# Attention with both batches' first blocks at the head of the order, feeding two feed-forward layers on one core

## The chip, the cores and the metric

The kernel runs on one core of a Trainium2 chip. The metric is the device time of one execution in microseconds; lower is better. All times below are of the kernel before, from its timed runs and from one profiled execution.

## The reference, cut to what matters

Attention over two batches of 768 tokens with 8 heads of 64; a query sees the 96 keys up to its own place and the first 8 keys of its batch, with a slope per head as bias. Its output goes through two feed-forward layers of width 512 to 2048 to 512, the first with a softplus, the second with `h * clip(h + 3, 0, 6) / 6`.

```python
def _attn_ref(q, k, v, n_global, n_local):
    scores = scale * np.matmul(q, k.transpose(0, 1, 3, 2))
    is_global = pos[None, :] < int(n_global)
    is_local = (rel >= 0) & (rel < int(n_local))
    keep = is_global | is_local
    dist = np.where(is_global & ~is_local, float(n_local), np.abs(rel))
    scores = np.where(keep, scores - slopes * dist, -1000000000.0)
    a = np.exp(scores - np.max(scores, axis=-1, keepdims=True))
    return np.matmul(a / (np.sum(a, axis=-1, keepdims=True) + 1e-09), v)

def _moe_ref(x, w_in, w_out):
    h = x @ w_in
    return (np.maximum(h, 0.0) + np.log1p(np.exp(-np.abs(h)))) @ w_out

def _moe2_ref(x, w_in, w_out):
    h = x @ w_in
    return (h * np.clip(h + 3.0, 0.0, 6.0) / 6.0) @ w_out
```

## The kernel before, in words

The weights come as 64-bit words and are turned on the chip into a high and a low part, so that three matmuls (low by high, high by low, high by high) give one product. The tokens are cut into 12 blocks of 128, 6 of each batch (`NB`).

*Attention* goes block by block, and a block in two quads of four heads each, so there are 24 quads (k = 0 to 23). A quad has three steps. `att_s` (L494) makes the scores on PE (L519), adds the bias and takes the row minimum of the negated scores on DVE (L525), takes the exponentials with their sums on ACT (L530), and normalises on POOL (L415). `att_t` (L539), twice in a quad, transposes two heads on PE (L553) and copies the result out of its PSUM bank on ACT (L555); from the sixth quad on there is one such bank. `att_v` (L558) multiplies with the values on PE (L571); after a block's second quad it splits the result into `xsh` and `xsl` (ACT L578, DVE L579), the input of the first layer.

The first block of a batch (i = 0) needs only its own keys, so its scores are 128 wide. Every other block needs its own and the previous block's, 256 wide. The keys of three blocks are kept in `kT`, slot n % 3. The first 32 keys of a batch are global: `att_s` copies them at the first block into `gk` (DVE, L503), and copies them from there over the first 32 columns of a block's slot when that block is done (L536), so that the next block finds them in its "previous" slot. The values do the same by a transfer (L584). At a block's first quad, `load_block` (L442) issues the transfers of the next block's queries and keys, and `load_values` (L448) those of its own values, all on SP's queue.

*The lead* (L657) does the first steps with LEAD = 5: the scores of quads 0 to 6, the transposes of 0 to 4, the values of 0 to 3. It also issues matmuls that compute nothing (`warm_up`) and converts six units of weights (`weight_step`, L155; `unit_convert`, L124). A unit's conversion starts with an absolute value on ACT (L140), goes over POOL and DVE, and ends with a subtraction on DVE (L153). Its work buffer `a` is one of the four quarters of the third partial-sum tile `part[2]`, or one of two buffers `wa` (L134 to L138); in the order of the units they go round in sixes.

*The halves* follow in `Layers.run` (L350). An item of the first layer (256 tokens, two chunks of weights) has two halves of 24 matmuls: `first_h` makes `hf`, `first_g` the softplus, `first_o` the product into `accf`. Between the matmuls of a half the steps of attention quads are issued, those of two quads in the first half, of one in each later half: scores and values ahead of the half's first matmul, transposes ahead of the 6th and of the 18th. The order of the items is fixed; the first ones are the first 256 tokens (two blocks), then the next 256. When the attention is done, its pools are closed and the rest of the two layers runs in items of 512 tokens (`item`, `last_items`), which write the output rows (L306, L329).

PE's instructions are in the order in which the program issues them. Those of ACT, DVE and POOL, with a few exceptions, are put in order by a planner at build time, from its own estimates.

## Time and profile before

| | us |
|---|---|
| median of 3 runs | 647.71 (647.69 to 648.22) |
| profiled execution | 649.05 |
| its span on the core | 647.1 |

The page gives for the whole span the busy time of each engine:

| engine | busy us | share |
|---|---|---|
| PE | 624.8 | 97% |
| PEld (weight loads, beside PE) | 513.8 | 79% |
| DVE | 428.9 | 66% |
| ACT | 375.1 | 58% |
| POOL | 151.0 | 23% |

A busy share is a mean over stages that are limited by different things. The views to read are therefore those by stretch of time, and the waits inside a stretch. A row of the timeline says when an instruction started, how long it took, and in brackets how long its engine was idle before it and what ended that.

### The profile page before, as it was taken

To read this page: it belongs to the slowest core of one execution; us is meant where nothing else is said; L and a number is where in the kernel's file an instruction comes from. 1 tells how busy PE (TensorE), PEld (TensorE's weight loads), DVE (VectorE), ACT (ScalarE), POOL (GpSimd) and SP (SyncE) were. 2 spreads that over 40 slices of the span, in tenths; PEclk is the share of its full clock that TensorE was granted. 3 is DMA by queue.
4 is the path that set the end of the run, shared out by engine and by line. 5 is a ranking of instruction groups with operands and counts; after the bars stand their busy time and mean duration, and the time that the engine had idled before them with its cause. 6 is when DMAs were issued, how large, how long until landed. Compare 5 with 4: busy or idle time off the path is not lost.

```text
span 647.1 us, 9643 instructions
## 1 busy us (share of the span) xinstructions
PE 624.8 (97%) x3495; PEld 513.8 (79%) x3496; DVE 428.9 (66%) x903; ACT 375.1 (58%) x786; POOL 151.0 (23%) x192
## 2 busy tenths in 40 slices
PE   7779998999999999999999999999999999999996
PEld 4567887889999888877788888888888888888885
DVE  7988587645799999999989995225833432424251
ACT  6866878674778887686787752326685222222230
POOL 4786364521133234443200400001100000000000
PEclk9989999999999999999999999999999999999999
DMA  8754222011134234433302032000462000001011
GB/s 285 238 158 147 70 75 62 23 25 66 66 116 146 98 130 131 130 99 129 122 10 66 32 131 98 0 1 32 134 208 82 0 1 0 2 1 65 1 66 69
DMA packets 25082, 53.67 MB, mean 83 GB/s; under 512 B 2497, under 2 KB 9153, under 8 KB 25025
## 3 DMA queue, kind: packets, MB, share of 16 engines
q1 hardware_dynamic: 25024, 52.96, 25.3%
q8 instruction: 29, 0.48, 0.3%
q14 instruction: 29, 0.23, 0.1%
HBM read 49.81 MB, written 3.15 MB: 82 GB/s over the span
## 4 chain that ended last, share of the span: by engine, by line
PE 68%; DVE 16%; ACT 7%; POOL 3%; DMA 3%; issue 2%; SPq 0%; ACTq 0%; DVEq 0%
PE acc L200 25%; PE h L200 24%; PE accf L200 6%; PE hf L200 5%; ACT pm L530 3%; PE accz L200 2%; PE hz L200 2%; DVE wa L147 2%; DVE wa L148 2%; PE ptp L553 2%; DVE w L153 2%; POOL wa L143 1%; POOL pm L415 1%; DVE pm L525 1%; DVE part L296 1%
## 5 line engine op out<-in xcount | busy, mean ns | idle before, releaser
L200 PE MATMUL h<-xsh,w 128*128 128x512 f32 x584 | 159.3, 396 | 0.4 <-DVE t L186 0.4
L200 PEld LDWEIGHTS h<-xsh,w 128*128 128x128 f32 x584 | 109.2, 188 | 27.6 <-DVE t L186 1.6
L143 POOL TENSOR_SCALAR wa<-wa 128x512 f32<-128x512 f32 x56 | 74.2, 1329 | 242.4 <-ACT wa L140 242.1
L200 PE MATMUL acc<-w,gh 128*128 128x512 f32 x344 | 108.0, 395 | 0.0
L190 DVE SCALAR_TENSOR_TENSOR t<-t,h 128x512 f32<-128x512 f32 x43 | 29.5, 686 | 81.7 <-ACT t L189 81.7
L200 PE MATMUL h<-xsl,w 128*128 128x512 f32 x292 | 82.4, 395 | 0.0
L192 DVE TENSOR_TENSOR gl<-t,gh 128x512 fp32r<-128x512 f32 x73 | 51.8, 709 | 43.1 <-ACT gh L191 42.8
L189 ACT ACTIVATE t<-h,three 128x512 f32<-128x512 f32 x43 | 29.5, 686 | 87.6 <-PE h L200 87.4
L200 PE MATMUL acc<-gh,w 128*128 128x512 f32 x240 | 78.9, 396 | 0.3 <-DVE part L296 0.2
L200 PEld LDWEIGHTS acc<-w,gh 128*128 128x128 f32 x344 | 64.5, 188 | 15.7
L191 ACT CAST gh<-t 128x512 fp32r<-128x512 f32 x73 | 45.2, 619 | 46.0 <-PE acc L200 22.0
L200 PE MATMUL acc<-w,gl 128*128 128x512 f32 x172 | 68.0, 396 | 0.0
L200 PEld LDWEIGHTS h<-xsl,w 128*128 128x128 f32 x292 | 54.8, 188 | 13.2
L415 POOL TENSOR_SCALAR pm<-pm,rs 128x256 f32<-128x256 f32 (+1 forms) x96 | 54.0, 580 | 37.6 <-DVE rs L413 18.3
L200 PE MATMUL accf<-ghf,w 128*128 128x256 f32 x288 | 58.7, 288 | 0.4 <-ACT ghf L191 0.4
L200 PEld LDWEIGHTS acc<-gh,w 128*128 128x128 f32 x240 | 44.9, 188 | 11.9 <-DVE part L296 0.6
L530 ACT ACTIVATE pm<-pm,nm 128x256 f32<-128x256 f32 (+1 forms) x96 | 46.1, 481 | 10.4 <-DVE nm L525 7.7
L200 PEld LDWEIGHTS accf<-ghf,w 128*128 128x128 f32 x288 | 46.5, 188 | 2.1 <-issue 1.2
L200 PE MATMUL acc<-gl,w 128*128 128x512 f32 x120 | 47.5, 396 | 0.0
L153 DVE TENSOR_TENSOR w<-wa,w 128x512 fp32r<-128x512 f32 x56 | 39.2, 700 | 9.7 <-ACT w L105 8.4
L200 PE MATMUL hf<-xsh,w 128*128 128x256 f32 x288 | 45.3, 288 | 0.0
L140 ACT ACTIVATE wa<-raw 128x512 f32<-128x512 f32 x53 | 35.5, 673 | 13.7 <-DVE w L153 6.4
(116 smaller groups left out, 1050.9 us busy)
## 6 DMA issues: line engine op xcount, KB each, us to landing
raw<-in_w2i SPq DMA_DIRECT2D x16, 512.0 KB, 3.3
raw<-in_w2o SPq DMA_DIRECT2D x16, 512.0 KB, 3.3
raw<-in_w1i SPq DMA_DIRECT2D x14, 512.0 KB, 3.7
raw<-in_w1o SPq DMA_DIRECT2D x12, 512.0 KB, 3.3
V<-in_v SPq DMA_DIRECT2D x12, 256.0 KB, 3.2
chk<-in_q SPq DMA_DIRECT2D x12, 256.0 KB, 2.8
chk<-in_k SPq DMA_DIRECT2D x12, 256.0 KB, 2.8
qT<-in_qt SPq DMA_DIRECT2D x11, 256.0 KB, 3.9
```

The costliest lines, as they stand in the source:

```text
L140: first = nc.scalar.activation(a, raw.bitcast(F32)[:, :, 1], AF.Abs)
L143: nc.gpsimd.tensor_scalar(out=a, in0=a, scalar1=W_HI, scalar2=W_LO, op0=ALU.min, op1=ALU.max)
L147: nc.vector.scalar_tensor_tensor(out=ai, in0=hi, scalar=-2 ** 30, in1=ai, op0=ALU.bitwise_and, op1=ALU.bitwise_or)
L148: nc.vector.scalar_tensor_tensor(out=ai, in0=lo, scalar=29, in1=ai, op0=ALU.logical_shift_right, op1=ALU.bitwise_or)
L153: nc.vector.tensor_tensor(out=wl, in0=a, in1=r32(wh), op=ALU.subtract)
L189: nc.scalar.activation(t1, hf, AF.Relu, bias=self.three[:, 0:1])
L190: nc.vector.scalar_tensor_tensor(out=t3, in0=t1, scalar=6.0, in1=hf, op0=ALU.min, op1=ALU.mult)
L191: nc.scalar.copy(gh, t3)
L192: nc.vector.tensor_tensor(out=gl, in0=t3, in1=r32(gh), op=ALU.subtract)
L200: return self.nc.tensor.matmul(out, lhsT=a, rhs=b, start=start and z == 0, stop=stop and z == len(seq) - 1, **kw)
L415: nc.gpsimd.tensor_scalar(out=t, in0=t, scalar1=rs[:, j:j + 1], scalar2=0.0, op0=ALU.mult, op1=ALU.add)
L530: nc.scalar.activation(pmz, pmz, AF.Exp, bias=nm[:, z:z + 1], scale=-1.0, accum_out=sm[:, z:z + 1])
```

## The change

The blocks are done in the order 0, 6, 1 to 5, 7 to 11 (`ORDER`), so that the first blocks of both batches come first. `z` is now the place of a block in that order and `n` its number. Block 6 gets a fourth slot in `kT` and keeps it until block 7 has read it; the other blocks share three slots, counted without block 6. Each batch has its own `gk`. The values of block 6 are loaded into the fourth quarter of `part[2]`, which therefore no longer serves as a work buffer for weights: these go round in fives. The rows of the output follow the order through `rows`.

```diff
--- before.py
+++ after.py
@@ -42,6 +42,7 @@
 SQ_LIMIT = 1.0e9
 W_LO = 2.0 ** -15
 W_HI = 122864.0
+ORDER = [0, NB, *range(1, NB), *range(NB + 1, 2 * NB)]
 SLOPES = [2.0 ** (-8.0 * (h + 1) / H) for h in range(H)]
 
 
@@ -59,6 +60,7 @@
     def __init__(self, ctx, tc, weights, xsh, xsl, out):
         self.ctx, self.tc, self.nc = ctx, tc, tc.nc
         self.weights, self.xsh, self.xsl, self.out = weights, xsh, xsl, out
+        self.rows = range(T // P)
         self.pool("mp", 2)
         self.pool("tp", 5)
         self.pool("pp", 1)
@@ -131,8 +133,8 @@
             self.W[j] = [wp.tile([P, CW], F32R, tag=f"w{i}_{t}", name=f"w{i}_{j}") for i in range(4)]
         raw = self.raws.pop(x)
         hi, lo = raw[:, :, 1], raw[:, :, 0]
-        z = self.home(x, 6)
-        if z < 4:
+        z = self.home(x, 5)
+        if z < 3:
             a = self.part[2][:, z, :]
         else:
             a = self.wr[x % len(self.wr)].tile([P, CW], F32, tag="wa", name=f"wa{j}_{u}")
@@ -303,7 +305,7 @@
                 continue
             nc.vector.scalar_tensor_tensor(out=pm, in0=acc, scalar=1.0 / 6.0, in1=pm, op0=ALU.mult, op1=ALU.add)
             if last_ph:
-                t0 = G * GB + m * P
+                t0 = self.rows[G * GB // P + m] * P
                 nc.sync.dma_start(out=self.out[t0:t0 + P, :], in_=pm)
 
     def last_items(self, ph, G, spare_step):
@@ -326,7 +328,7 @@
                 spare_step()
         for m in range(4):
             acc = self.bank(self.acc_tags[m], f"accz{m}")
-            t0 = G * GB + m * P
+            t0 = self.rows[G * GB // P + m] * P
             ms = slice(m * P, (m + 1) * P)
             for cs in (slice(0, 512),) if m < 3 else (slice(0, 256), slice(256, 512)):
                 for s, (gh, gl) in enumerate(g):
@@ -422,7 +424,7 @@
         nc = tc.nc
         xsh, xsl = x_tiles(ctx, tc)
         layers = Layers(ctx, tc, weights, xsh, xsl, out)
-        layers.beside = True
+        layers.beside, layers.rows = True, ORDER
         tp = layers.tp
         layers.room = actx.enter_context(tc.tile_pool(name="ap_r", bufs=1))
         ap2 = actx.enter_context(tc.tile_pool(name="ap2", bufs=3))
@@ -433,20 +435,27 @@
         ps_s = actx.enter_context(tc.tile_pool(name="ps_s", bufs=1, space=PSUM))
         ps_t = actx.enter_context(tc.tile_pool(name="ps_t", bufs=1, space=PSUM))
         ps_x = actx.enter_context(tc.tile_pool(name="ps_x", bufs=1, space=PSUM))
-        kT = ap1.tile([P, KC, 3, P], F32, name="kT")
-        gk = ap1.tile([P, KC, MAX_GLOBAL], F32, name="gk")
+        kT = ap1.tile([P, KC, 4, P], F32, name="kT")
+        gk = [ap1.tile([P, KC, MAX_GLOBAL], F32, name=f"gk{b}") for b in range(B)]
         qT, V, px = {}, {}, {}
         zeros = ap1.tile([P, 512], BF16, name="zeros")
         nc.vector.memset(zeros, 0.0)
+
+        def slot_of(n):
+
+            return 3 if n == NB else (n - n // NB) % 3
 
         def load_block(n):
             qT[n] = ap2.tile([P, KC, P], F32, tag="qT", name=f"qT{n}")
             for cs in (slice(0, 1), slice(1, KC)) if n == 0 else (slice(0, KC),):
                 nc.sync.dma_start(out=qT[n][:, cs], in_=qt[n][:, cs])
-                nc.sync.dma_start(out=kT[:, cs, n % 3, :], in_=kt[n][:, cs])
+                nc.sync.dma_start(out=kT[:, cs, slot_of(n), :], in_=kt[n][:, cs])
 
         def load_values(n):
-            V[n] = [ap_v.tile([P, DM], F32, tag="V", name=f"V{n}")]
+            if n == NB:
+                V[n] = [layers.part[2][:, 3, :]]
+            else:
+                V[n] = [ap_v.tile([P, DM], F32, tag="V", name=f"V{n}")]
             nc.sync.dma_start(out=V[n][0], in_=v[n * P:(n + 1) * P, :])
             if n % NB:
                 V[n].append(V[n - 1][0])
@@ -493,21 +502,22 @@
 
         def att_s(k):
 
-            n, e = divmod(k, KC // 2)
-            i, slot = n % NB, n % 3
+            z, e = divmod(k, KC // 2)
+            n = ORDER[z]
+            i, slot, first = n % NB, slot_of(n), gk[n // NB]
             if e == 0:
-                if n + 1 < B * NB:
-                    load_block(n + 1)
+                if z + 1 < B * NB:
+                    load_block(ORDER[z + 1])
                 load_values(n)
                 if i == 0:
-                    nc.vector.tensor_copy(gk, kT[:, :, slot, 0:MAX_GLOBAL])
-            before = (n - 1) % 3
+                    nc.vector.tensor_copy(first, kT[:, :, slot, 0:MAX_GLOBAL])
+            before = slot_of(n - 1) if i else slot + 1
             w = P if i == 0 else 2 * P
             nsl = w // P
             mo = 2 if i == 0 else 0
             step = before - slot
             end = slot + nsl * step
-            ks = slice(slot, min(end, 3) if end >= 0 else None, step)
+            ks = slice(slot, min(end, 4) if end >= 0 else None, step)
             two = layers.acc_tags if k < LEAD and k % 2 else s_tags
             ps = [layers.bank(t, f"s{k}_{j}", (P, 2, 2, P)) for j, t in enumerate(two)]
             pm = ap_m.tile([P, 4, 2 * P], F32, tag="pm", name=f"pm{k}")
@@ -533,13 +543,13 @@
             rs = ap_m.tile([P, 4], F32, tag="rs", name=f"rs{k}")
             softmax_rows(nc, sm, rs, [pm[:, z, 0:w] for z in range(4)])
             if e == KC // 2 - 1 and 1 <= i < NB - 1:
-                nc.vector.tensor_copy(kT[:, :, slot, 0:MAX_GLOBAL], gk)
+                nc.vector.tensor_copy(kT[:, :, slot, 0:MAX_GLOBAL], first)
             pms[k] = pm
 
         def att_t(k, a):
 
-            n, e = divmod(k, KC // 2)
-            nsl = 1 if n % NB == 0 else 2
+            z, e = divmod(k, KC // 2)
+            nsl = 1 if ORDER[z] % NB == 0 else 2
             pm = pms[k] if a == 0 else pms.pop(k)
             pt_shape = [P, 2, 2, P]
             if k < LEAD and a:
@@ -557,7 +567,8 @@
 
         def att_v(k):
 
-            n, e = divmod(k, KC // 2)
+            z, e = divmod(k, KC // 2)
+            n = ORDER[z]
             i = n % NB
             nsl = 1 if i == 0 else 2
             if e == 0:
@@ -574,7 +585,7 @@
                         ))
             if e < KC // 2 - 1:
                 return
-            g, o = divmod(n * P, GB)
+            g, o = divmod(z * P, GB)
             nc.scalar.copy(xsh[g][:, :, o:o + P], px[n])
             nc.vector.tensor_tensor(
                 out=xsl[g][:, :, o:o + P], in0=px[n], in1=r32(xsh[g][:, :, o:o + P]), op=ALU.subtract
```

## Rows read from the trace of the kernel before

**Rows 1.** The page, part 4: the chain that ended last, by engine, shares of the span
```profile
PE 68%; DVE 16%; ACT 7%; POOL 3%; DMA 3%; issue 2%; SPq 0%; ACTq 0%; DVEq 0%
```

**Rows 2.** Busy by stretch: us, then PE, PEld, DVE, ACT, POOL busy (count), clock, DMA
```profile
0.00:31.00 31.00, 24.47 (x167) 14.26 (x168) 25.70 (x111) 24.58 (x83) 18.13 (x39) 1.00 0.80 263
31.00:42.00 11.00, 7.45 (x72) 6.24 (x73) 10.93 (x34) 6.21 (x20) 10.83 (x15) 0.99 0.66 192
57.00:76.00 19.00, 18.60 (x178) 16.80 (x178) 11.24 (x42) 13.63 (x41) 9.61 (x18) 1.00 0.32 102
```

**Rows 3.** Waits of PE, 31 to 151 us: who, for whom, us, times, longest
```profile
PE ptp L553 <- ACT pT L555: 8.0, 12, 2.8
```

**Rows 4.** Groups by line and form, 0 to 150 us: busy, mean ns | idle before
```profile
L530 ACT ACTIVATE pm<-pm,nm 128x256 f32<-128x256 f32 x80 | 39.9, 500 | 10.4 <-DVE nm L525 7.7 <-POOL pm L415 1.8 <-POOL t2f L181 0.7
...
L530 ACT ACTIVATE pm<-pm,nm 128x128 f32<-128x128 f32 x16 | 6.2, 387 | 0.0
...
L555 ACT COPY pT<-ptp 128x512 f32<-128x512 f32 x40 | 23.0, 577 | 14.2 <-PE ptp L553 14.2
...
L555 ACT COPY pT<-ptp 128x256 f32<-128x256 f32 x8 | 2.7, 358 | 1.2 <-PE ptp L553 1.2
...
L525 DVE CUSTOM_DVE_ANT_0 pm<-s,bias 128x256 f32<-128x256 f32 x80 | 29.4, 417 | 12.7 <-PE s L519 12.7
...
L525 DVE CUSTOM_DVE_ANT_0 pm<-s,bias 128x128 f32<-128x128 f32 x16 | 3.7, 286 | 2.7 <-PE s L519 2.7
```

**Rows 5.** Timeline of DVE: start, us, instruction, count [idle before <- what ended it]
```profile
16.64 0.17 DVE L412 TENSOR_SCALAR rs<-sm 128x4 f32<-128x4 f32 x1 [1.13 <-ACT pm L530]
```

**Rows 6.** Timeline of PE in the halves, 58 to 134 us
```profile
58.65 1.13 PE L519 MATMUL s<-kT,qT 64*128 64x256 f32 x8
...
64.64 0.72 PE L519 MATMUL s<-kT,qT 64*128 64x128 f32 x8
...
72.92 0.60 PE L553 MATMUL ptp<-ident,pm 128*128 128x128 f32 x4
...
76.01 1.13 PE L519 MATMUL s<-kT,qT 64*128 64x256 f32 x8
...
77.08 1.09 PE L571 MATMUL px<-pT,V 128*64 128x128 f32 x16
...
78.92 0.38 PE L553 MATMUL ptp<-ident,pm 128*128 128x128 f32 x2
...
83.24 0.66 PE L571 MATMUL px<-pT,V 128*64 128x128 f32 x8
...
93.76 1.14 PE L519 MATMUL s<-kT,qT 64*128 64x256 f32 x8
...
101.11 1.13 PE L519 MATMUL s<-kT,qT 64*128 64x256 f32 x8
...
133.77 1.13 PE L519 MATMUL s<-kT,qT 64*128 64x256 f32 x8
```

**Rows 7.** Timeline of PE and DVE, 42 to 54 us
```profile
42.03 1.09 PE L553 MATMUL ptp<-ident,pm 128*128 128x128 f32 x4 [2.83 <-ACT pT L555]
...
49.04 0.23 DVE L503 COPY gk<-kT 128x128 f32<-128x128 f32 x1 [0.66 <-DMA kT<-in_kt]
...
53.31 0.39 PE L200 MATMUL accf<-ghf,w 128*128 128x256 f32 x1 [0.44 <-ACT ghf L191]
```

**Rows 8.** The page, part 6: a load, count, size, us from issue to landing
```profile
qT<-in_qt SPq DMA_DIRECT2D x11, 256.0 KB, 3.9
```

**Rows 9.** Weight steps by line, to 160 us: ns min/median/max, first and last start
```profile
L153 DVE TENSOR_TENSOR w<-part,w x8: 655/698/1092, 24.1 to 94.3; 128x512 fp32r<-128x512 f32 x8
...
L140 ACT ACTIVATE wa<-part x3: 673/674/694, 29.7 to 114.1; 128x512 f32<-128x512 f32 x3
```

**Rows 10.** Busy by stretch, as rows 2, two short stretches of the start
```profile
28.00:32.00 4.00, 2.23 (x26) 1.57 (x24) 4.00 (x8) 2.40 (x7) 3.92 (x5) 1.00 0.62 196
...
42.00:45.30 3.30, 3.27 (x16) 2.86 (x16) 0.96 (x1) 2.06 (x4) 3.18 (x6) 0.51 0.34 130
```

## What I expect of the change, and why

> **What bounds the kernel now.** I read the whole-program views first and then go into the start, where the change lies. The chain of work that ended last belongs to PE for 68% of the span, and DVE is next with 16% [rows 1]. So a change gains only by taking time from the part where PE waits, or by taking work from PE. PE's work is the same before and after: every block is still computed, only at another place. In such a case the whole question is how much PE waits.
>
> The busy table by stretch tells where it waits [rows 2]. In the first 31 us PE is busy for 24.47, and the warm-up matmuls, which compute nothing, are among them. From 31 to 42 us it is busy for 7.45 of 11, while DVE is busy for 10.93 of 11: here the conversion of weights and the softmax share DVE, and PE waits for them. From 57 to 76 us PE is busy for 18.60 of 19. So there are two regimes: a lead of some 42 us in which ACT, DVE and POOL set the pace, and from there halves of layer-1 items with one attention quad each, in which PE sets it, with short waits. The waits of the second regime have one cause: 8.0 us in 12 waits, the second pair of transposes of a quad waiting for ACT to copy the first pair out of their single PSUM bank; 2.8 of them are one wait [rows 3].
>
> **What the change moves.** A first block has no block before it, so its scores are 128 wide where others are 256. The second batch's first block (block 6) now takes the place of block 1 in the lead, and blocks 1 to 5 come one place later. Quads 2 and 3 become narrow, quads 12 and 13 become wide. Nothing is removed in sum but one stall, below.
>
> *The lead.* Of quads 2 and 3, eight exponentials shrink from 500 to 387 ns, 0.9 us of ACT; four copies of transposes shrink from 577 to 358 ns, 0.9 us more; eight DVE score steps shrink from 417 to 286 ns, 1.0 us; POOL's eight normalising steps shrink too [rows 4], but POOL is idle for 12.9 of the first 31 us [rows 2], so nothing is counted for them. What reaches the end of the lead is less than the sum, because the engines take turns. DVE's row at 16.64 us [rows 5] is the turning point: it waits there 1.13 us for ACT's exponentials of quad 3, and the DVE score steps of quads 2 and 3 are already done. Those exponentials (0.9 us less before that point) move the turning point. From there on DVE is full [rows 2], with the same work in both kernels, so the shorter copies behind it gain only where DVE also gets its weight steps earlier. The bounds are 0.9 and 1.8 us; I take 1.2, near the lower end, since the full DVE is the row nearest to it.
>
> *The halves.* Quads 12 and 13 now cost PE their full price beside the layer's matmuls: eight score matmuls take 1.13 us where the narrow ones took 0.72; sixteen value matmuls 1.09, eight 0.66; four transposes 0.60, two 0.38, twice in a quad [rows 6]. That is 0.41 + 0.43 + 0.44 = 1.3 us for a quad, 2.6 us for two. The stretch concerned is five halves, from 64.64 to 93.76 us, 29.12 us. A full half without a wait is the one from 58.65 to 64.64, 5.99 us; five of them are 29.95, 0.8 us more than now (the extra work would then fill waits that are there). The five full halves from 101.11 to 133.77 us have a mean of 6.53; five of those would be 32.65, 3.5 us more [rows 6]. Bounds 0.8 and 3.5; I take 2.6, the work itself, with the waits left as they are.
>
> *The stall that goes.* Block 6 copies its first 32 keys into the single buffer `gk` with a DVE instruction. In the kernel before it is queued at 48.4 us, and DVE waits 0.66 us for the key transfer to land and then copies for 0.23 [rows 7]. Behind it in DVE's queue stand the steps of layer 1's first activation; ACT's cast and the first output matmuls wait for those, and PE is idle 0.44 us at 53.31 us [rows 7]. After, batch 2 has its own `gk` buffer and the copy is in the lead. The gain is between 0 (something else is late next: the transposes' wait for ACT) and 0.89; I take 0.8, as DVE is full up to that cast. The same copy, moved into the lead, is a wait added to DVE at about 6 to 10 us, with the first score steps and bias steps behind it, and ACT's exponentials waiting for these. Its bounds are 0, if the keys have landed, and again 0.89; I take 0, because DVE waits for ACT between 11 and 17 us anyway (1.13 us at the turning point alone [rows 5]).
>
> *What costs nothing.* The loads are the same in number and size; a block's load takes 3.9 us to land [rows 8] and is issued a block ahead, in the halves two of 5.99 us [rows 6]. On SP's queue the key load of block 2 no longer waits for an earlier quad, since the fourth slot makes room; the key load of block 3 waits instead, one block later, as the rotation of three did. Block 6's values go to the fourth quarter of the third partial-sum tile, which the weights give up. The weights then go round five work buffers instead of six: the sixth unit's first step (29.7 us) needs the buffer whose last reader (the first subtraction, 24.1 us) is some 5 us earlier [rows 9], so some 4.5 us of cover are left after that instruction, whose longest took 1.09 us, and both ends of it move together with the lead. If it were gone, ACT's queue would stop at that step with the exponentials behind it. The rows of the output are written elsewhere, in transfers of the same size.
>
> **The sum.** -1.2 (lead) + 2.6 (halves) - 0.8 (stall) = +0.6 us. The profiled execution took 649.05 us, for a span of 647.1; a like execution after would take 649.65. The median of the runs shown is 1.34 us lower, 647.71, so the forecast is 648.3.
>
> **The clock.** At 42.03 us PE comes out of its wait of 2.83 us [rows 7], and from 42.0 to 45.3 us the granted clock is 0.51, the lower of its two levels, 1.2 GHz [rows 10]; PE is busy for the whole of it and does half its work, 1.6 us lost. I count this as unchanged: DVE's row that causes the wait keeps its place behind the weight steps. From 28 to 32 us PE was busy for only 2.23 of 4 us and the clock stayed at 1.00 [rows 10]. The Trainium skill (TensorE: Matmul & The Clock Gate, "What's actually happening") says that the lower clock is the default and that activity releases it; this speaks against the change, which takes matmuls out of the lead. The trace agrees that idling was followed by the low clock once, at 42 us, and shows that thinner work alone, as at 28 us, was not. That gives one of the rivals.
>
> **Rivals.**
> - *The lead gives all of it back, and the wait at 42 us closes.* If the weight steps come early enough on DVE, the lead ends 1.8 us earlier, and the low clock behind the wait (1.6 us) goes. For it: DVE idles 1.13 us just before it is full, and the whole wait hangs on DVE's order. Against it: DVE's load from 31 to 42 us is untouched. -1.8 - 0.8 - 1.6 + 2.6 = -1.6: 646.1, faster by 0.25%.
> - *The widened halves go at the pace of the later ones.* The exponentials and copies of quads 12 and 13 lengthen ACT's queue in each of those halves, and the second pair of transposes waits for its copy [rows 3]. This decides from the point at which ACT's copy of the first pair ends after PE's 18th matmul of the half; the later halves are past it, the one at 58.65 is not. Then +3.5, and the stall's gain is lost in the same wait: 3.5 - 1.2 = +2.3: 650.0, slower.
> - *The lead doesn't get shorter.* The change doesn't do what it says if transfers or weights set the lead: -0 + 2.6 - 0.8 = +1.8: 649.5, slower. Against it: ACT is busy for 24.58 of 31 us [rows 2] and has exponentials or copies in all of the first half.
> - *The clock falls once more in the lead or at the first halves*, as PE has 2.6 us less to do there. The price is that of the stretch at 42 us, 1.6 us: +0.6 + 1.6 = +2.2: 649.9. Only one stretch of the start shows it, behind a full stop of 2.83 us.
>
> **How the numbers follow.** About 0.2%, 1.3 us, is what a measurement of this kernel can tell from no change. The forecast has 0.48; the first rival 0.22; the halves at the later pace 0.16; no shorter lead 0.07; the clock 0.07. Only the first is faster, and the last three are all slower by more than 1.3 us, so 0.22 faster, 0.48 the same, 0.30 slower. The likeliest case's own range is 646.8 to 649.0. The range that should hold 8 times in 10 reaches from a little under the first rival (its stall gain at the upper bound, and some of the 2.83 us of idling with it), 645.7, to the halves at the later pace, with 0.3 for the moved copy, 650.3. The order of instructions on ACT, DVE and POOL is chosen anew by a planner for the changed program, and that alone may move a wait of the lead by as much as the terms above; this is why the range isn't narrower.
>
> **What would show it.** The lead: quad 2 and 3's exponentials at 387 ns, DVE's turning point at about 15.8 instead of 16.64 us, the first long PE wait ending about 41 us instead of 42.03. The halves: the five from 64.64 us take 31 to 32 us instead of 29.12. The stall: no DVE wait for a key transfer at 49 us, and a copy into the second `gk` before 12 us without a wait. The clock: one low stretch of 3.3 us, no more and no less. The prediction is wrong if the lead ends over 2 us earlier, if the low clock goes away or comes twice, or if the five halves stay under 30 us.

## The result, and the profile after

The changed kernel takes 652.25 us (652.02 to 652.58) where the kernel before, beside it, takes 647.85. The ratio is 1.0066, with an interval of 1.0049 to 1.0083: 4.3 us slower, where 648.3 was forecast and 650.3 was the upper end. The profiled execution took 652.58 us, its span is 650.4, 3.3 more than before. Its line numbers are 2 to 11 higher: L412 is now L414, L525 is L535, L144, L147 and L148 are L146, L149 and L150, L503 is L513.

The chain that ended last, by engine, answers to [rows 1]:

```profile
PE 65%; DVE 17%; ACT 8%; DMA 5%; issue 3%; POOL 1%; SPq 0%; ACTq 0%; DVEq 0%
```

Busy by stretch, with the columns of [rows 2]: the same three stretches, then three short ones as in [rows 10].

```profile
0.00:31.00 31.00, 23.69 (x137) 13.18 (x140) 24.70 (x109) 21.72 (x79) 16.13 (x37) 0.94 0.79 263
31.00:42.00 11.00, 9.84 (x80) 7.70 (x78) 10.60 (x33) 6.50 (x22) 9.77 (x14) 0.84 0.50 154
57.00:76.00 19.00, 18.59 (x173) 16.37 (x173) 13.12 (x46) 14.46 (x40) 8.46 (x14) 1.00 0.31 96
...
14.00:17.50 3.50, 3.17 (x17) 2.04 (x16) 1.84 (x11) 2.60 (x11) 3.09 (x9) 0.51 1.05 384
31.00:34.50 3.50, 3.50 (x25) 2.42 (x23) 3.50 (x10) 1.76 (x7) 2.98 (x5) 0.52 0.24 61
44.70:48.20 3.50, 3.50 (x25) 2.66 (x24) 1.53 (x10) 2.89 (x8) 3.09 (x6) 0.51 0.00 1
```

The granted clock falls to its lower level three times, at 14, 31 and 45 us; before, the start shows it once, at 42 us [rows 10]. PE's longer busy time from 31 to 42 us, 9.84 against 7.45 [rows 2], is partly this: the same matmuls take twice as long.

Waits of PE over the whole span (who for whom, us, times, longest), and the groups by form, answer to [rows 3] and [rows 4]:

```profile
PE ptp L563 <- ACT pT L565: 6.0, 8, 2.6
PE ptp L563 <- POOL pm L417: 3.3, 3, 1.8
```

```profile
L540 ACT ACTIVATE pm<-pm,nm 128x128 f32<-128x128 f32 x16 | 6.2, 389 | 0.3 <-DVE nm L535 0.3
...
L565 ACT COPY pT<-ptp 128x256 f32<-128x256 f32 x8 | 2.7, 364 | 1.1 <-PE ptp L563 1.1
```

The narrow exponentials and copies have the durations that the sum used. But PE now waits 3.3 us for POOL's normalised exponentials, where it waited 1.1 us before, in as many waits. The order of DVE tells why; first after, then the rows of before that stand at the same place:

```profile
7.72 0.23 DVE L513 COPY gk<-kT 128x128 f32<-128x128 f32 x1 [0.61 <-DMA kT<-in_kt]
...
10.99 0.17 DVE L414 TENSOR_SCALAR rs<-sm 128x4 f32<-128x4 f32 x1
...
16.56 0.49 DVE L414 TENSOR_SCALAR rs<-sm 128x4 f32<-128x4 f32 x1 [1.50 <-ACT pm L540]
...
17.19 0.40 DVE L146 TENSOR_SCALAR part<-part 128x512 int32<-128x512 int32 x1
17.61 0.74 DVE L149 SCALAR_TENSOR_TENSOR part<-part,part 128x512 int32<-128x512 int32 x1
18.39 0.74 DVE L150 SCALAR_TENSOR_TENSOR part<-part,part 128x512 int32<-128x512 int32 x1
19.06 0.41 DVE L535 CUSTOM_DVE_ANT_0 pm<-s,bias 128x256 f32<-128x256 f32 x1
```

```profile
9.54 0.16 DVE L412 TENSOR_SCALAR rs<-sm 128x4 f32<-128x4 f32 x1
...
16.94 0.40 DVE L144 TENSOR_SCALAR part<-part 128x512 int32<-128x512 int32 x1
17.25 0.42 DVE L525 CUSTOM_DVE_ANT_0 pm<-s,bias 128x256 f32<-128x256 f32 x1
```

Three things have moved. The copy of block 6's first keys stands ahead of the first score step and waits 0.61 us for its transfer. Quad 0's normaliser stands behind three of the four score steps of quad 2, 10.99 us instead of 9.54. And behind the turning point (16.56 us, not the 15.8 that was forecast) the planner does all three conversion steps of the first weight unit before it begins quad 4's scores, at 19.06 instead of 17.25. PE pays for the last of the three some microseconds later:

```profile
25.07 1.14 PE L529 MATMUL s<-kT,qT 64*128 64x256 f32 x8 [1.73 <-issue]
...
28.59 0.90 PE L563 MATMUL ptp<-ident,pm 128*128 128x128 f32 x4 [1.79 <-POOL pm L417]
...
30.75 1.77 PE L529 MATMUL s<-kT,qT 64*128 64x256 f32 x8
...
43.62 0.63 PE L563 MATMUL ptp<-ident,pm 128*128 128x128 f32 x4 [2.55 <-ACT pT L565]
...
52.28 1.14 PE L529 MATMUL s<-kT,qT 64*128 64x256 f32 x8
...
59.37 1.13 PE L529 MATMUL s<-kT,qT 64*128 64x256 f32 x8
...
65.37 1.13 PE L529 MATMUL s<-kT,qT 64*128 64x256 f32 x8
...
97.16 1.14 PE L529 MATMUL s<-kT,qT 64*128 64x256 f32 x8
...
104.41 1.14 PE L529 MATMUL s<-kT,qT 64*128 64x256 f32 x8
...
136.25 1.14 PE L529 MATMUL s<-kT,qT 64*128 64x256 f32 x8
```

The scores of the same quads give the balance. At 52.28 the kernel is 1.57 us behind (50.71 before), where the lead should have put it 1.2 ahead. The half that follows has lost its stall and takes 7.09 us instead of 7.94, so at 59.37 the kernel is 0.72 behind (58.65 before [rows 6]), where the prediction had it 2.0 ahead. The five halves from 65.37 take 31.79 us instead of 29.12, 2.67 more. The five from 104.41 to 136.25 take 31.84, 0.8 less than before (32.66). That leaves 2.5 us at 136 us; the last 0.8 come after the attention, where the profiled executions of these kernels, all with the same work there, lie between 496.2 and 499.0 us (497.4 before, 498.2 after).

### The profile page after: what moved, and what is told of

Same layout as the page of the kernel before. It is cut to its first block, busy times and chain, and to the rows that moved or that the text cites. A ratio compares the mean times of both kernels' runs of the same rounds, so it can differ in the third digit from the quotient of the medians.

```text
span 650.4 us, 9644 instructions
## 1 busy us (share of the span) xinstructions
PE 629.1 (97%) x3495; PEld 516.0 (79%) x3496; DVE 429.2 (66%) x903; ACT 376.0 (58%) x786; POOL 147.5 (23%) x192
## 4 chain that ended last, share of the span: by engine, by line
PE 65%; DVE 17%; ACT 8%; DMA 5%; issue 3%; POOL 1%; SPq 0%; ACTq 0%; DVEq 0%
PE acc L202 21%; PE h L202 20%; PE accf L202 7%; PE hf L202 6%; ACT pm L540 3%; DMA chk<-in_q 3%; PE ptp L563 2%; DVE wa L150 2%; DVE wa L149 2%; PE accz L202 2%; PE hz L202 2%; PE px L582 2%; DVE w L155 2%; PE s L529 2%; DVE gl L194 1%
## 5 line engine op out<-in xcount | busy, mean ns | idle before, releaser
L145 POOL TENSOR_SCALAR wa<-wa 128x512 f32<-128x512 f32 x56 | 71.1, 1273 | 246.9 <-ACT wa L142 246.9
L540 ACT ACTIVATE pm<-pm,nm 128x256 f32<-128x256 f32 (+1 forms) x96 | 46.1, 482 | 11.8 <-DVE nm L535 11.8
L142 ACT ACTIVATE wa<-raw 128x512 f32<-128x512 f32 x56 | 37.5, 673 | 13.4 <-DVE w L155 6.9
L535 DVE CUSTOM_DVE_ANT_0 pm<-s,bias 128x256 f32<-128x256 f32 (+1 forms) x96 | 33.0, 395 | 17.5 <-PE s L529 17.5
```

The source lines that it names most:

```text
L142: first = nc.scalar.activation(a, raw.bitcast(F32)[:, :, 1], AF.Abs)
L145: nc.gpsimd.tensor_scalar(out=a, in0=a, scalar1=W_HI, scalar2=W_LO, op0=ALU.min, op1=ALU.max)
L535: nc.vector.tensor_tensor_reduce(out=pmz, in0=ps[z % 2][:, z // 2, 0:nsl, :].rearrange("p s t -> p (s t)"), in1=bias[:, 4 * e + z, mo:mo + ...
L540: nc.scalar.activation(pmz, pmz, AF.Exp, bias=nm[:, z:z + 1], scale=-1.0, accum_out=sm[:, z:z + 1])
```

## The experiments

Each ratio is to the kernel before on the same chip; 0.001 is 0.65 us. Four theories stand against each other: the loss comes from the *work* in the lead and the halves, at the prices of the sum; from the *planner's new order*; from the *clock*; or from the *storage*.

**One part of the work at a time.** In the kernel before, with its own storage: block 1 narrow, as if it had no block before it (its scores against block 0 are left out); block 6 wide (it attends to a block too much); and both.

```diff
+        def alone(n):
+            return n % NB == 0 or n == 1     # block 6 wide: n == 0; both: n < 2
-            w = P if i == 0 else 2 * P
+            w = P if alone(n) else 2 * P
```

> The kernel before, in its order, but block 1 attends only its own keys (left out: its previous block), so quads 2 and 3 are narrow in the lead as in the changed kernel, and nothing gets wider elsewhere. It prices the lead alone. By the prediction's step the lead ends 0.9 to 1.8 us earlier: 1.2 us faster than before. Rival (the lead doesn't get shorter: DVE is full of weight steps, and the planner puts the normaliser of quad 0 behind more score steps): 0 to 0.5 us faster, or slower where the clock falls once more. If PE were the limit in the lead, it would be 2.6 us faster.

> The kernel before, in its order, but block 6 also goes over the block before it (a part of the computation that the reference does not have), so quads 12 and 13 are wide in the halves as in the changed kernel. It prices the halves alone. By the prediction's step 2.6 us slower than before, with 0.8 and 3.5 as bounds; the five halves from 64.6 us take 31.7 us instead of 29.1. Rival (waits absorb the work): 0.8 us.

> Both at once: block 1 narrow (its previous block left out) and block 6 wide (a block too much), in the old order with the old storage. It has the changed kernel's widths without its second key buffer, its moved copy, its fourth key slot and its five work buffers; the wait for block 6's keys at 49 us is still there. By the prediction's steps 2.6 - 1.2 = 1.4 us slower than before. If the lead gains nothing, 2.6 slower. If the changed kernel's loss has a further cause in storage, this stays well under its 4.3 us.

Measured: 1.0012 (1.0002 to 1.0022), 1.0042 (1.0028 to 1.0055) and 1.0059 (1.0047 to 1.0071). The widened block costs 2.7 us (1.8 to 3.6), where 2.6 was forecast; in its trace the five halves from 65.38 us take 31.78 instead of 29.12, and the five later ones give 0.8 back, as in the changed kernel. The narrowed block, which takes work out of the lead and adds none, makes the kernel 0.8 us *slower*. Both together are 3.8 us slower: nearly the whole loss of the change, without its storage and without its copies.

**The copies and the storage.** The changed kernel without the copy of block 6's first keys; the kernel before with a copy of block 1's first keys into an unused tile at the same place; the changed storage with the blocks in the old order; and the second `gk` alone, filled late, so that the stall at 49 us [rows 7] goes and nothing moves into the lead.

```diff
# changed kernel without the copy
-            i, slot, first = n % NB, slot_of(n), gk[n // NB]
+            first = gk[0] if n < NB else kT[:, :, 3, 0:MAX_GLOBAL]
# kernel before with one copy more
+                if n == 1:
+                    nc.vector.tensor_copy(scratch, kT[:, :, slot, 0:MAX_GLOBAL])
# changed storage, old order
-ORDER = [0, NB, *range(1, NB), *range(NB + 1, 2 * NB)]
+ORDER = list(range(2 * NB))
# kernel before, second gk filled late
+            if n == NB and e == KC // 2 - 1:
+                tc.keep_in_program_order(nc.vector.tensor_copy(gk[1], kT[:, :, slot, 0:MAX_GLOBAL]))
```

> The changed kernel without the second batch's key copy: block 6 keeps its slot of kT for good, so later copies read the 32 keys from that slot, and DVE's instruction that waited 0.61 us for the key transfer ahead of quad 0's score steps is not there. Theory 1 (the moved copy starts the loss of the lead): quad 0's score steps begin at about 7.1 us instead of 7.86, POOL's first normalising step about 0.8 us earlier, and the kernel is 0.8 us or more faster than the changed one, 651.4 or less; if the low clock of 14 to 17 us was a consequence of that delay it goes too, and the time is near 649.8. Theory 2 (the low clock comes from the matmuls taken out of the lead, whatever the copy does): two extra low stretches stay, and no more than 0.8 us is gained, 651.4. Rival 3 (the lead doesn't matter, the loss is in the halves alone): no gain, 652.2.

> The kernel before, order and all, with one DVE copy more: the first 32 keys of block 1 into a tile that nothing reads, as the changed kernel does with block 6's keys; it stands in DVE's queue at the same place, ahead of quad 0's score steps. It adds the moved wait alone. Theory 1: DVE waits about 0.6 us for the transfer there and the kernel is 0.3 to 0.9 us slower than before, 648.2 to 648.8, and more if the clock falls an extra time behind it. Theory 2: the clock falls no more often than before, since no matmul has left the lead; at most 0.9 us. Rival 3: no difference, since ACT and DVE have slack between 11 and 17 us.

> All of the change's storage with the old order: four slots of kT, two gk buffers, block 6's values in the partial-sum tile, five work buffers for the weights instead of six, but the blocks in the order 0 to 11. If the storage costs (the work buffer, or the planner's order that comes with it), it is slower than before by over 1 us. By all theories the loss comes with the order: within 0.8 us of before, 647 to 648.6, perhaps 0.8 us faster, as the wait for block 6's keys at 49 us is gone if its keys come early.

> The kernel before with a second key buffer whose copy is pinned behind quad 13's steps, so that DVE no longer waits for block 6's keys at 49 us, and nothing else moves. It prices the stall that the change takes away. By the prediction's step 0.8 us faster than before, with 0 and 0.9 as bounds; the half from 50.7 to 58.7 us takes about 7.1 us instead of 7.94. Rival (the transposes' wait for ACT is late next): no difference.

Measured: 1.0047 (1.0032 to 1.0062); 1.0021 (1.001 to 1.0031); 1.0034 (1.0023 to 1.0045); 1.0009 (0.9995 to 1.0022). Without the copy the changed kernel is still 3.1 us slower, so the copy isn't the main cause; the 1.2 us between the two lie within the error of both. One copy more in the lead of the kernel before costs 1.4 us, more than its 0.23 us and its wait of 0.63; the section on the hardware shows a wait that came with it. The storage alone costs 2.2 us in the old order of the blocks. There the planner put the copy into the second `gk` forward into the full lead, where DVE waits for the keys, and PE then waits 2.07 us for DVE at 23.04 us:

```profile
21.38 0.23 DVE L513 COPY gk<-kT 128x128 f32<-128x128 f32 x1 [2.23 <-DMA kT<-in_kt]
```

Whether this row is the whole 2.2 us wasn't tested by itself. The stall, taken away by itself, gains nothing that the times show, though the half that had it is 0.84 us shorter in the trace (50.72 to 57.82 instead of 50.71 to 58.65).

**More warm-up.** The changed kernel with 28 matmuls that compute nothing between the first quads instead of 12, against the falls of the clock.

```diff
-WARM, FILL = 12, (6, 4, 2, 0, 0)
+WARM, FILL = 12, (10, 4, 2, 4, 8)
```

> The changed kernel with more matmuls that compute nothing in the lead: 10, 4, 2, 4, 8 instead of 6, 4, 2, 0, 0 for the five steps, 16 more at 0.22 us each, 3.5 us of PE work put where PE waited for POOL (1.05 us at 12.1 us, 1.79 us at 28.6 us) or DVE. Theory 2: the clock stays high there; of the three low stretches (14.0, 31.1 and 44.8 us) one or two go, each worth up to 1.6 us where PE is the limit: 649.5 to 651. Theory 1 and rival 3: no gain, since the added matmuls only fill or lengthen PE's queue: 652 to 653.

Measured: 1.0065 (1.0052 to 1.0078). Its profiled execution shows one low stretch instead of three, but that is the best of five: its mean clock is 0.996 and its time 652.02, the other four have 0.992 or 0.993, as the changed kernel has, and 652.76 to 653.25. So the warm-ups didn't keep the clock up in most executions, and they are PE work themselves. The run doesn't decide what the clock costs.

**The order held.** The first 130 instructions of DVE (128 in the changed kernel without the copy), 110 of ACT and 66 of POOL are chained in the order in which the kernel before runs them; the chains add no waits between engines. Four kernels: block 1 narrow; block 1 narrow and block 6 wide; the changed kernel without the copy; and, for the clock alone, the kernel before without its 12 warm-ups between the quads.

```diff
+        for engine, ranks in ORDER_OF.items():
+            traced = [i for i in nc.cur_bb.bb.instructions if i.engine == getattr(mybir.EngineType, engine)]
+            traced.sort(key=lambda i: int(i.name[2:]))
+            for x, y in zip(ranks, ranks[1:]):
+                tc.add_manual_dep(traced[y], traced[x].name, ...)
```

> The kernel before with block 1 narrow (its scores against block 0 are left out), as in the run before it, but with the instructions of the lead on DVE (the first 130), ACT (110) and POOL (66) held in the order in which the kernel before runs them. The lead has less work and nothing stands in another place. Theory 'the planner's new order eats the lead's gain': 0.9 to 1.2 us faster than the kernel before (the run without the held order was 0.8 us slower than it), the turning point on DVE near 15.8 us and the score steps of quad 4 on DVE before 17 us. Theory 'the clock falls more often with less work on PE': 0 to 1 us slower than the kernel before, with two or three low stretches of the granted clock before 50 us where the kernel before shows one. Theory 'the lead is set by something else, such as transfers': within 0.3 us of the kernel before and the turning point at 16.5 us or later.

> The kernel before with block 1 narrow and block 6 wide (one block of keys left out, one too much), the lead's instructions held in the order of the kernel before. Without the held order this was 3.8 us slower than the kernel before. Theory 'planner's order': 1.5 us slower (2.7 for the widened halves, 1.2 back from the lead). Theory 'clock': 3 to 4 us slower, as without the held order. Theory 'lead set by something else': 2.7 us slower.

> The changed kernel without the copy of block 6's first keys (they are read where they lie), with the lead's instructions on DVE, ACT and POOL held in the order of the kernel before. Without the held order it was 3.1 us slower than the kernel before. Theory 'planner's order': 2.7 for the halves less 1.2 for the lead, 1.5 us slower, perhaps 0.7 if the stall that goes is worth its 0.8 after all. Theory 'clock': some 3 us slower, as without the held order. Theory 'storage' (the fewer buffers for weights or the transfers of block 6 cost something of their own): slower than the kernel with block 1 narrow and block 6 wide in the same held order by 0.5 us or more.

> The kernel before without the 12 warm-up matmuls that stand between the first quads (the warm-ups ahead of the first quad stay), the order on DVE, ACT and POOL held. The work on DVE, ACT and POOL is that of the kernel before; PE alone has some 2.6 us less to do in the lead. Theory 'the clock falls more often with less work on PE': 0.5 to 2 us slower, one or two low stretches of 3.4 us more before 42 us. Theory 'planner's order' and theory 'something else sets the lead': within 0.3 us of the kernel before, since PE's own work in the lead is not what sets it.

Measured: 0.9991 (0.9982 to 1.0); 1.002 (1.0009 to 1.0031); 1.0009 (0.9996 to 1.0022); 1.0015 (1.0002 to 1.0028). With nothing changed but the order, the three kernels gain 1.4, 2.5 and 2.5 us. That is the planner's order, and it is the largest term of the miss. (The kernel before under its own chains wasn't run; with block 1 narrow, DVE's instructions follow its order one by one in the trace, up to 58 us.) The lead's gain comes back, but smaller than forecast: 0.6 us directly (0 to 1.2), 1.4 as the difference between the widened block alone (2.7) and both (1.3). The widened block costs 1.9 us here, as the difference between both and block 1 narrow, less than the 2.7 above: the five halves take 2.9 us more (63.48 to 95.54 against 63.19 to 92.32), and the five later ones 0.7 less. Without the warm-ups, in the same order, the kernel is 1.0 us slower (0.1 to 1.8), with a mean granted clock of 0.993 in its timed executions against 0.996.

The held order also shows what keeps the turning point where it was. ACT and DVE with block 1 narrow, order held:

```profile
14.46 0.68 ACT L145 ACTIVATE part<-part 128x512 f32<-128x512 f32 x1 [0.64 <-DMA part<-in_w1i]
15.05 0.39 ACT L538 ACTIVATE pm<-pm,nm 128x128 f32<-128x128 f32 x1
```

```profile
16.71 0.17 DVE L417 TENSOR_SCALAR rs<-sm 128x4 f32<-128x4 f32 x1 [2.42 <-ACT pm L538]
...
17.01 0.40 DVE L149 TENSOR_SCALAR part<-part 128x512 int32<-128x512 int32 x1
17.32 0.42 DVE L533 CUSTOM_DVE_ANT_0 pm<-s,bias 128x256 f32<-128x256 f32 x1
```

ACT is done early with the narrow exponentials and then waits 0.64 us for a transfer of *weights*, whose absolute value stands ahead of quad 3's exponentials in its queue. The time saved on ACT is given to that transfer, and the turning point stays at 16.71 (16.64 before [rows 5]). Of the seven kernels of this document with narrow quads 2 and 3 whose order is held, in whole or in part, six wait for this transfer, 0.15 to 0.96 us, and the turning point lies between 16.40 and 17.05. Whether ACT waits hangs on when the transfer has landed: in the profiled execution of both blocks changed, in the planner's order, ACT doesn't wait for it, and the turning point comes at 15.73, where the prediction had it:

```profile
15.73 0.42 DVE L412 TENSOR_SCALAR rs<-sm 128x4 f32<-128x4 f32 x1 [1.37 <-ACT pm L533]
```

That kernel is 3.8 us slower all the same, with the three weight steps behind this row.

**Which place in the order.** Block 1 narrow, held as above on ACT and POOL, and on DVE but for one place: first only the normaliser of quad 0, behind quad 2's scores; then the whole part from the turning point on in the planner's new order, at its head the three weight steps ahead of quad 4's scores. Both lists are shortened.

```diff
-    'DVE': [..., 34, 29, 37, 39, 30, 38, 40, 35, ...],
+    'DVE': [..., 34, 37, 39, 38, 29, 40, 30, 35, ...],     # the normaliser, 29 and 30
-    'DVE': [..., 43, 62, 64, 63, 44, 65, 47, 68, 45, ...],
+    'DVE': [..., 43, 44, 45, 62, 64, 63, 47, 65, 68, ...], # the weight steps, 43 to 45
```

> The kernel before with block 1 narrow (its scores against block 0 are left out), the lead held in the order of the kernel before on ACT and POOL, and on DVE too but for one place: the two normaliser steps of quad 0 stand behind quad 2's score steps, as the planner puts them for the narrow block. With everything held this was 0.6 us faster than the kernel before, with the planner's own order 0.8 slower. If the normaliser's place is what costs: 0.4 to 0.8 us slower than the kernel before. If the weight steps' place is: 0.6 us faster still. In the trace quad 0's normaliser would stand near 10.5 us instead of 9.5, POOL's first normalising step one us later, and quad 3's exponentials with it.

> The same, with the other place changed: the normaliser of quad 0 as in the kernel before, and DVE from the turning point at 16 us on in the order that the planner chooses for the narrow block, with the three conversion steps of the first weight unit ahead of quad 4's score steps. If the weight steps' place is what costs: 0.4 to 0.8 us slower than the kernel before, quad 4's scores at 18 us or later, PE's wait for its transposes near 28 us longer. If the normaliser's place is: 0.6 us faster.

Measured: 0.9995 (0.9985 to 1.0006) and 1.004 (1.0027 to 1.0053). The normaliser's place costs nothing that can be seen. The order from the turning point on costs 3.2 us against the held order. DVE and PE of the second:

```profile
17.13 0.74 DVE L152 SCALAR_TENSOR_TENSOR part<-part,part 128x512 int32<-128x512 int32 x1
17.91 0.74 DVE L153 SCALAR_TENSOR_TENSOR part<-part,part 128x512 int32<-128x512 int32 x1
18.57 0.41 DVE L533 CUSTOM_DVE_ANT_0 pm<-s,bias 128x256 f32<-128x256 f32 x1
```

```profile
24.61 1.14 PE L527 MATMUL s<-kT,qT 64*128 64x256 f32 x8 [1.75 <-issue]
...
27.70 0.90 PE L561 MATMUL ptp<-ident,pm 128*128 128x128 f32 x4 [1.37 <-POOL pm L420]
...
44.73 1.08 PE L561 MATMUL ptp<-ident,pm 128*128 128x128 f32 x4 [3.77 <-ACT pT L563]
```

Quad 4's scores begin at 18.57 instead of 17.32. Its exponentials and POOL's normalising follow, PE's transposes wait for these, and each later quad inherits the delay. The cost is larger here than that of the planner's whole order against the held one (1.4); that ACT and POOL were held in an order that doesn't fit this one may be the reason, and wasn't tested. The three weight steps weren't moved alone either: the run prices the order from the turning point on, and the rows show what stands at its head. The same rows in the changed kernel (17.19 to 19.06, 25.07 and 28.59 us) point to the same place.

**The changed kernel whole, order held.** With the copy of block 6's first keys where the planner had put it, and with the copy at 11.8 us, where DVE waits for ACT.

```diff
-    'DVE': [..., 19, 37, 21, 23, ..., 35, 36, 42, ...],     # the copy, 37, ahead of the first scores
+    'DVE': [..., 19, 21, 23, ..., 35, 36, 37, 42, ...],     # behind quad 2's normaliser
```

> The changed kernel whole, with the copy of block 6's first keys at the head of the score steps as the planner has it, the rest of the lead held in the order of the kernel before. Without the copy this order was 0.6 us slower than the kernel before (the changed kernel in its own order: 4.3 slower). If the copy costs its wait for the transfer and its own time at that place: 0.9 to 1.3 us more than without it, so 1.5 to 1.9 us slower than the kernel before. If the held order takes the cost up in DVE's waits for ACT between 11 and 16 us, as the prediction had it: 0.6 us slower.

> The changed kernel whole, the lead held as in the run before this one, but with the copy of block 6's first keys moved to where DVE waits for ACT's exponentials anyway, behind quad 2's normaliser at about 11.3 us. If the copy costs only by its place: as without the copy, 0.6 us slower than the kernel before, and a DVE row of the copy without a wait for a transfer. If the fourth slot and its transfers cost by themselves: 1.2 us or more slower.

Measured: 1.0008 (0.9997 to 1.0018) and 1.0016 (1.0006 to 1.0027). The same program as the changed kernel, in the old order, is 0.5 us slower than the kernel before instead of 4.3. The copy costs nothing that can be told in either place (without it 1.0009). DVE and PE in the first of them:

```profile
16.58 0.25 DVE L419 TENSOR_SCALAR rs<-sm 128x4 f32<-128x4 f32 x1 [1.74 <-ACT pm L545]
...
17.27 0.42 DVE L540 CUSTOM_DVE_ANT_0 pm<-s,bias 128x256 f32<-128x256 f32 x1
```

```profile
28.24 1.13 PE L534 MATMUL s<-kT,qT 64*128 64x256 f32 x8
...
57.83 1.13 PE L534 MATMUL s<-kT,qT 64*128 64x256 f32 x8
...
63.85 1.14 PE L534 MATMUL s<-kT,qT 64*128 64x256 f32 x8
...
95.91 1.13 PE L534 MATMUL s<-kT,qT 64*128 64x256 f32 x8
```

These rows give the place of the loss in the changed program itself. The turning point stands at 16.58 here and at 16.56 in the planner's order, so up to there nothing is lost by the order. Behind it quad 4's scores begin at 17.27 instead of 19.06, and quad 7's on PE at 28.24 instead of 30.75 (28.13 in the kernel before). At 57.83 it is 0.82 us ahead of the kernel before [rows 6], then loses 2.9 us in the five halves (32.06 instead of 29.12) and wins 0.8 back in the five later ones.

**The change turned round.** If a narrow block is worth 2.7 us in the halves and about 1 in the lead, it should pay to take block 0 *out* of the lead: order 1 to 7, 0, 8 to 11, with block 0's keys and values kept; once with the planner's order, once with the old one held.

```diff
-ORDER = [0, NB, *range(1, NB), *range(NB + 1, 2 * NB)]
+ORDER = [*range(1, NB + 2), 0, *range(NB + 2, 2 * NB)]
```

> The change turned round: block 0 is taken out of the lead and done after block 7 (order 1 to 7, 0, 8 to 11), so that both narrow blocks lie beside full halves; its keys and values are kept till then. From the runs before: a narrow block is worth 2.7 us in the full halves and some 0.6 to 1.2 us in the lead. With the planner's own order: the two halves that get block 0 take 1.3 us less each, 2.6 in sum; the lead gets 0.6 to 1.8 us longer, and the first scores wait for one transfer of keys more. 1 us faster than the kernel before if the planner leaves the first weight unit's steps behind quad 4's scores, 1 to 2 us slower if it does not.

> The same with the lead held in the order of the kernel before (the first 112 places on DVE, with the copy of the global keys into block 1's slot behind quad 1's scores; 100 on ACT, 66 on POOL). 0.8 to 2 us faster than the kernel before if a narrow block's worth is what the runs showed (2.7 in the halves, 0.6 to 1.2 in the lead); no faster if the longer start of the lead, two blocks' keys and a copy between quads 1 and 2, costs over 1.5 us.

Measured: 1.0041 (1.0027 to 1.0056) and 1.0059 (1.0038 to 1.008). DVE and PE at the start of the second, in which POOL's list has 60 places and not the 66 of the expectation:

```profile
7.86 0.23 DVE L522 COPY gk<-kT 128x128 f32<-128x128 f32 x1 [2.40 <-DMA kT<-in_kt]
```

```profile
7.90 1.57 PE L538 MATMUL s<-kT,qT 64*128 64x256 f32 x12 [0.97 <-DMA kT<-in_kt]
...
12.99 2.08 PE L538 MATMUL s<-kT,qT 64*128 64x256 f32 x8 [3.53 <-DVE kT L555]
```

From quad 7's scores (34.22 us, 28.13 before) to the last values of the attention (151.36, 149.74 before) it wins back 4.5 us, so the halves do gain. But the lead is 6.1 us longer. DVE waits 2.40 us for the keys at its start, and block 2's scores must now wait until DVE has copied the global keys into block 1's slot, a step that stands in a chain at once instead of two quads later. The price in the lead was taken from the width alone and left this out. The held order gains nothing here; the two times lie within the error of both. No version that computes the whole attention beat the kernel before.

## Why the prediction was wrong, point by point

**The lead, -1.2: wrong in sign, and the main cause.** Two steps of the argument failed. First, the prediction treated the order of DVE's queue as given: its last sentence on the range says that the planner orders anew and may move a wait "by as much as the terms above", but that stands as a reason for width, without a place, a price or a chance. It should have been a rival. The price is 3.8 us: 4.3 for the changed kernel, 0.5 for the same program in the old order. Its place is the order from the turning point on: the changed program stands there at 16.56 us in the one order and at 16.58 in the other, and they part where the first weight unit's steps and quad 4's scores compete for a full DVE. That these steps alone carry the loss wasn't tested. Narrowing block 1 is enough to make the planner choose the weights there, as the profile of that kernel shows (the steps at 16.72, 17.15 and 17.92 us, its turning point at 16.04). Second, "those exponentials move the turning point" holds only where a weight transfer ahead of quad 3's exponentials has landed: in the old order ACT waits for it, and the turning point is at 16.71. The rival "transfers or weights set the lead" was right in this, at a chance of 0.07. The step behind it failed too: where the turning point did come at 15.73, in the planner's order, nothing of it was left at quad 11's scores, 58.66 us against 58.65. The first long wait of PE, which should have ended about 41 us, ended at 43.62. What the old order does gain, 0.6 to 1.4 us, shows only behind 42 us. With block 1 narrow there is no low clock there in the profiled execution (41.5 to 45.5 us at 1.00, where before has 0.51 [rows 10]), but its timed executions have a lower mean clock than before, 0.994 against 0.996, which speaks against the clock as the reason. It stays open.

**The halves, +2.6: right for the five halves, but a term is missing behind them.** They cost 2.67 us by the rows of the changed kernel: the extra work of PE beside a PE that is full costs its own time. The five halves from 104.41 us then give 0.8 back, in the trace of every kernel whose quads 12 and 13 are wide, and of none where they are narrow; PE waits twice there for ACT's copies, 0.96 us, instead of five times, 1.70. The prediction had nothing for them. The net price by time is 1.9 us in the held order and 2.7 for the block widened alone, whose profiled lead was itself 1.5 us late at quad 7. Why the waits go stays open.

**The stall that goes, -0.8: seen in the trace, not in the times.** The half of the old stall takes 7.09 us instead of 7.94. Alone, the removal measured +0.6 us (-0.3 to +1.4). In the held order the changed kernel without its copy is 0.7 us faster than the kernel that has the same widths and the stall, within the error of both. Where the 0.8 go when nothing else changes isn't settled.

**The moved copy, 0: right by its reason in the old order, wrong as a claim on any lead.** In the changed program DVE does have slack there: with and without the copy, 1.0008 and 1.0009. In the kernel before the same copy costs 1.4 us.

**The clock, unchanged: wrong.** Three low stretches instead of one. The rival "the clock falls once more" named the right thing at 0.07, with 1.6 us for one stretch; measured, the low clock costs less in the lead. Taking the warm-ups away lowered the mean clock by 0.003 and cost 1.0 us. Kernels in the planner's new order have mean clocks of 0.991 to 0.992 in their timed executions, the same in the old order 0.994 to 0.995. Among the executions of one and the same kernel, over all the kernels timed here, a mean clock lower by 0.001 goes with 0.16 us more (0.11 to 0.21). By this the clock makes some 0.4 us of the 3.8, an estimate, since no run changed the clock alone; the rest would then be waits.

**The base: 1.0 us of the miss.** The prediction took 1.34 us off its forecast, since the profiled execution of before lay that far over the median. That of the changed kernel lay only 0.3 over its own. Against the profiled execution, 649.65 was forecast and 652.58 measured, 2.9 us; against the medians it is 4.0. This part is the spread of single executions and no cost of the change.

**The sum in the old order: right by luck.** The changed program in the old order is 0.5 us slower, and +0.6 was forecast. But at 57.83 us it is 0.82 us ahead and not 2.0, the five halves cost 2.9 and not 2.6, and the 0.8 won back behind them stood in no term.

## What to carry to other kernels

Where a planner orders a full engine's queue anew, the order is a term of the sum: look for the row at which two kinds of work compete for the engine that is full, and price the case in which they change places. A saving in front of such a row can be lost behind it, and holding the old order in the changed program is the experiment that separates the two. And before a saving is carried along a queue, look at what else stands in that queue with a wait of its own, such as a transfer.

## What the runs showed of the hardware

A small DVE copy between two SBUF tiles can be held up until POOL's work beside it ends. The copy of the global keys, 128 by 128, took 0.21 us at 22.92 us in the kernel before and 1.61 at 15.97 with one copy more. POOL, DVE and PE of the kernel before with one copy more:

```profile
13.78 2.56 POOL L415 TENSOR_SCALAR pm<-pm,rs 128x128 f32<-128x128 f32 x6
16.30 1.20 POOL L143 TENSOR_SCALAR part<-part 128x512 f32<-128x512 f32 x2
```

```profile
15.97 1.61 DVE L539 COPY kT<-gk 128x128 f32<-128x128 f32 x1
```

```profile
17.64 1.13 PE L522 MATMUL s<-kT,qT 64*128 64x256 f32 x8 [1.09 <-DVE kT L539]
```

The copy starts at 15.97 and ends at 17.58, 0.08 us after POOL's row ends at 17.50. In the kernel before it starts a microsecond earlier and gets through after 0.53 us, 0.08 after POOL's normalising row ends:

```profile
13.57 1.86 POOL L415 TENSOR_SCALAR pm<-pm,rs 128x256 f32<-128x256 f32 x4
...
14.98 0.53 DVE L536 COPY kT<-gk 128x128 f32<-128x128 f32 x1
```

The changed storage in the old order shows it too, 1.62 us, again 0.08 after POOL. The Trainium skill (SBUF — State Buffer, "Who interferes with whom") says that DVE in its two-port mode and POOL share a pair of ports, and that whoever comes second is blocked until the other's instruction ends. The trace agrees that the copy ends just behind an instruction of POOL; but where it took 1.61 us it stayed behind three POOL instructions in a row, and with block 1 narrow, order held, it got through in 0.29 us at 14.01, inside a row of POOL that goes on to 14.89. What decides between the two isn't shown.

PE's next scores wait 1.09 us for the held copy. That this wait makes most of the 1.4 us is likely, but it wasn't tried with POOL out of the way. The copy can be held without anything new ahead of it: with block 6 wide, and DVE's order that of the kernel before, it took 1.61 us at 15.57 in the profiled execution, the slowest of its six.
